# Every large matmul of an attention and FFN kernel split into two 64-row tiles that swap PSUM banks halfway

## The chip, the cores and the metric

The kernel runs on one core of a Trainium2 chip. The metric is the device time of one execution in microseconds, here the median of three runs. TensorE is called PE, VectorE DVE, ScalarE ACT, GpSimd POOL and SyncE SP, as in the profile.

## The reference

Block-sparse attention over 4 batches, 8 heads, 768 positions and a head dimension of 64, and after it a gated feed-forward layer over the 3072 tokens. Inputs and output are float32.

```python
scores = scale * np.matmul(q, k.transpose(0, 1, 3, 2))      # scale 1/8
# mask: neighbouring blocks of 32, first and last block, and 3 sampled blocks per block row
scores = np.where(mask, scores, -1e9)
scores = scores - np.max(scores, axis=-1, keepdims=True)
attn = np.exp(scores)
attn = attn / (np.sum(attn, axis=-1, keepdims=True) + 1e-09)
x = np.matmul(attn, v)                                        # heads joined: (3072, 512)
gate = 1.0 / (1.0 + np.exp(-(x @ w_gate)))                    # (512, 1536)
val = x @ w_val
out = (gate * val) @ w_out                                    # (1536, 512)
```

## The kernel before

The work is cut into 12 **units**: 4 batches times 3 groups of 256 query positions (`UQ`). All operands on PE are float16, all sums float32 in PSUM. PSUM has eight banks of 512 float32 columns.

**Attention of a unit.** Heads go in pairs, four pairs to a unit, and a pair has three steps (class `Step`). A step computes the scores of two heads for 256 keys and 256 queries, transposed, with keys on the partitions (`qk`, L460): four matmuls that contract over 64 rows, two for each head. The two heads lie on partitions 0 to 63 and 64 to 127, so each two matmuls use the two row halves of the PE array and write different PSUM banks. ACT takes the exponential of the two banks in one instruction (`exp`, L470), and DVE multiplies by the 0/1 mask (`mul`, L476). In the first unit the mask is added on PE as a bias instead (L452). `Pair.pv` (L498) multiplies the probabilities by the values, 24 matmuls of 65 columns for a pair, whose 65th column is the sum of the probabilities; DVE takes the reciprocal and scales (`norm`, L508 and L510). The result is transposed into `xT`, on PE in the first two units (L519), by a DMA transpose on SP's queue (L551) later.

**FFN of a unit** (class `Ffn`). `f` (L618) makes one of 12 chunks of 128 hidden features: four matmuls with the gate weights and four with the value weights, each contracting 128 rows, 256 columns, both in the two halves of one bank. ACT takes the tanh of the gate half (L629) and DVE forms (tanh + 1) times value (L634) into `ht`. `y` (L658) makes 128 tokens of the output in 12 matmuls of 512 columns; ACT (L695) copies them out with a factor 0.5 and SP's queue stores them. The very last tile goes out in two halves (`last`, L679 on ACT and L682 on DVE).

**The order.** The order of the instructions is made at build time by `Plan`: every piece of work is a task with the engines that may do it, a cost in microseconds written by hand, what it depends on, and the PSUM buffers that it takes and frees. `Plan.run` goes through time; whenever an engine is free it gives it the first ready task whose buffers are free, and so fixes the buffer too. The instructions are then issued in that order, and each engine runs its own list in order. A task that stands in the list waits for its semaphores, and all behind it on the same engine wait with it.

**PSUM.** There are two kinds of buffers, and the planner hands them out separately:

```python
plan = Plan({'m': 4, 's': 2})
spare = [ps.tile([128, 512], f32, name=f"m{i}") for i in range(4)]
score = [ps.tile([128, 2, 2, UQ], f32, name=f"s{i}") for i in range(2)]
```

The scores of a step take one of two `s` buffers of two banks; `pv`, `f`, `y`, the transposes and the mask tiles take one of four `m` buffers of one bank. The scores of two steps are issued together, except in the first two units (`scores`).

The FFN of a unit runs while the attention of the next unit is computed; their tasks are listed alternately in six slots (`parts`). At the start the queries, keys and values of batch 0 and then the FFN weights are loaded on POOL's queue, and the block mask is built: DVE and ACT copy mask tiles from PSUM (`mask_tile`, L348 and L235).

Of the kernel before, what the change touches and what calls it, by code (L numbers as in the profile page):

```python
# [25 lines left out]
DM = H * D  # L26
# [11 lines left out]
VW = 96  # L38

# [12 lines left out]
class Bank:  # L52
    def __init__(self, kind):
        self.kind, self.slot = kind, None


class Plan:
# [6 lines left out]
    def __init__(self, banks):  # L64
        self.tasks = []
        self.room = {kind: [(0.0, i) for i in range(n)] for kind, n in banks.items()}
# [5 lines left out]
    def run(self):  # L72
# [11 lines left out]
        while events:  # L84
            now, i = heapq.heappop(events)
            if i >= 0:
                for bank in self.tasks[i][5]:
                    self.room[bank.kind].append((now, bank.slot))
                for j in after[i]:
                    left[j] -= 1  # L90
                    if not left[j]:
                        bisect.insort(ready, j)
            if events and events[0][0] <= now:
                continue
            for eng in busy:
                if busy[eng] > now:
                    continue
                for j in ready:
# [4 lines left out]
                    kinds = [bank.kind for bank in take]  # L103
                    if any(len(self.room[x]) < kinds.count(x) for x in kinds):
                        continue
                    for bank in take:
                        oldest = min(self.room[bank.kind])
                        self.room[bank.kind].remove(oldest)
                        bank.slot = oldest[1]
# [5 lines left out]
                    order.append((eng, fn))  # L115
# [3 lines left out]
        for eng, fn in order:  # L119
            fn(eng)  # L120
        return end
# [3 lines left out]
def kernel(  # L125
# [132 lines left out]
    plan = Plan({'m': 4, 's': 2})  # L258
    spare = [ps.tile([128, 512], f32, name=f"m{i}") for i in range(4)]
    score = [ps.tile([128, 2, 2, UQ], f32, name=f"s{i}") for i in range(2)]  # L260
# [29 lines left out]
    def warm(n):  # L290
        for _ in range(n):
            nc.tensor.matmul(spare[3], junk[:, 0:128], junk, start=True, stop=True)
# [5 lines left out]
    bank = Bank("m")  # L298
# [24 lines left out]
    def more_rows():  # L323
        bank = Bank("m")
# [16 lines left out]
    def mask_tile(c0, c1, t):  # L341
        n = c1 - c0
        w = 512 // n
        bank = Bank("m")
# [21 lines left out]
    def prep(src, dst, b, p, t0, t1, deps, at):  # L366

        bank = Bank("m")
# [69 lines left out]
    class Step:  # L438
# [6 lines left out]
        def qk(self):  # L445
            b, u, p = self.b, self.u, self.p
            masked = (b, u) != (0, 0)
            for i in range(2):
                t = 2 * self.j + i
                if not masked:  # L450
                    for o in (0, D):
                        nc.tensor.matmul(  # L452
                            score[self.bank.slot][:, o // D, i, :],
                            e64[o : o + D, t * 128 : (t + 1) * 128],
                            bias[o : o + D, :],
                            start=True,
                            stop=False,
                        )
                for o in (0, D):
                    nc.tensor.matmul(  # L460
                        score[self.bank.slot][:, o // D, i, :],
                        kT[b % 2][o : o + D, p, t * 128 : (t + 1) * 128],
                        qT[b % 2][o : o + D, p, u * UQ : (u + 1) * UQ],
                        start=masked,
                        stop=True,
                    )

        def exp(self, eng):
            self.pt = work.tile([128, 2, 2, UQ], f16, tag="P", bufs=3 * VB, name="pt")
            nc.scalar.activation(  # L470
                self.pt, score[self.bank.slot], AF.Exp, bias=0.0, scale=SCALE
# [11 lines left out]
    class Pair:  # L483


        def __init__(self, n, p):
# [4 lines left out]
            self.bank, self.bank2 = Bank("m"), Bank("m")  # L491

        def pv(self, s):
            acc = spare[self.bank.slot][:, 0 : 4 * (D + 1)]
            self.acc = acc.rearrange("a (s h d) -> a s h d", s=2, h=2)
            for a in range(2):
                for t in range(NT):
                    nc.tensor.matmul(  # L498
                        self.acc[:, s, a, :],
                        self.steps[t // 2].pt[:, a, t % 2, s * 128 : (s + 1) * 128],  # L500
                        vex[self.b % 2][:, 2 * self.p + a, t, 0 : D + 1],
                        start=(t == 0),
                        stop=(t == NT - 1),
                    )

        def norm(self, eng):
# [4 lines left out]
                self.x16,  # L511
# [20 lines left out]
        def value(self):  # L532
            a = plan.add(
                [(PE, 0.41)],
                lambda eng: self.pv(0),
                self.products + [vdone[self.b, self.p]],
                take=[self.bank],
                lag=0.0,
            )
            a = plan.add([(PE, 0.41)], lambda eng: self.pv(1), [a])  # L540
# [30 lines left out]
    def scores(run):  # L571
# [10 lines left out]
        if first:  # L582
            deps.append(t_bias)
        a = plan.add(
            [(PE, 0.1 + (0.44 if first else 0.22) * len(run))],
# [14 lines left out]
    class Ffn:  # L600
# [7 lines left out]
        def f(self, f):  # L608
# [3 lines left out]
            def mm(eng):  # L612
                if f == 0:
                    self.ht = work.tile([128, NF, UQ], f16, tag="ht", bufs=2, name="ht")
                pg = spare[bank.slot].rearrange("a (i n) -> a i n", i=2)
                for i, w in enumerate((wg, wv)):
                    for c in range(4):
                        nc.tensor.matmul(  # L618
                            pg[:, i, :],
                            w[:, c, f * 128 : (f + 1) * 128],  # L620
                            xTs[self.n][0][:, c, :],
                            start=(c == 0),
                            stop=(c == 3),
                        )

            def tanh(eng):
                th = work.tile([128, UQ], f32, tag="th", bufs=4, name="th")
                box.append(th)
                nc.scalar.activation(  # L629
                    th, spare[bank.slot][:, 0:UQ], AF.Tanh, bias=0.0, scale=0.5  # L630
                )

            def gate(eng):
                nc.vector.scalar_tensor_tensor(  # L634
                    self.ht[:, f, :],
                    in0=box[0],
                    scalar=1.0,
                    in1=spare[bank.slot][:, UQ : 2 * UQ],
# [4 lines left out]
            deps = xdone[self.n] + (ring("ht", 2) if f == 0 else [])  # L643
            a = plan.add([(PE, 0.88)], mm, deps, at=land["w", f // 3], take=[bank])
            if f == NF - 1:
                used["xT"].append(a)
            c = plan.add([(ACT, 0.36)], tanh, [a] + ring("th", 4))
# [255 lines left out]
```

## Time and profile before

| | |
|---|---|
| runs | 297.08, 297.65, 297.1 us; median 297.1 us |
| span of the profiled execution | 294.5 us; 2.6 us less than the median, and no total of its own is recorded |
| granted TensorE clock | 0.999 |
| PE | 287.0 us busy, 3302 matmuls |
| ACT | 205.2 us busy, of it 139.8 us in 144 exponentials (L470) |
| DVE | 191.2 us busy, of it 91.0 us in 132 mask products (L476) |
| DMA | 28.55 MB read, 6.29 MB written |

The span runs from the first to the last instruction of the trace; the timed runs also hold what lies around it. Busy PE time is counted from modelled ends of pipelined matmuls that overlap, so the rows of the chain (start, length, engine, line, number of instructions) are the better guide: they follow PE from one start to the next.

### The profile page before, as it was taken

The page shows a single profiled execution, that of the slowest core. Times are in us where ns is not written, and L with a number is a line of the kernel's source. Part 1 is how long each engine was busy: PE and PEld are TensorE (multiplying, and loading weights), DVE is VectorE, ACT ScalarE, POOL GpSimd, SP SyncE. Part 2 cuts the span into 40 slices and gives each one's busy share as a digit, 9 for nine tenths or more (in the row PEclk, how much of TensorE's full clock was granted, in tenths as well). Part 3 has the DMA queues.
Part 4 walks back from the last instruction along what each step waited for, and adds up shares of the span by engine and source line. Part 5 has one row for each costly group of instructions (what it writes and reads, how often), then busy time and mean ns, then how long its engine had stood idle before and what let it go on. Part 6 is the DMA issues. An engine that isn't in the chain of part 4 may idle for free.

```text
span 294.5 us, 7862 instructions
## 1 busy us (share of the span) xinstructions
PE 287.0 (97%) x3302; PEld 203.8 (69%) x3302; DVE 191.2 (65%) x439; ACT 205.2 (70%) x323; POOL 48.3 (16%) x65
## 2 busy tenths in 40 slices
PE   7998999999999999999999999999999999999994
PEld 2656785785785786786776786786686687687771
DVE  3688878775675677675676577577477477475240
ACT  2789977677677677677677677777777777672431
POOL 8944100197000000197000000000000000000000
PEclk9999999999999999999999999999999999999999
DMA  7999999999910200999910203910200200201102
GB/s 115 190 201 204 205 206 203 215 150 146 222 16 23 79 11 10 191 171 143 220 24 12 81 11 70 214 43 20 80 11 20 80 11 20 80 13 20 71 2 71
DMA packets 74540, 28.55 MB, mean 97 GB/s; under 512 B 57352, under 2 KB 71560, under 8 KB 74504
## 3 DMA queue, kind: packets, MB, share of 16 engines
q0 software_dynamic: 40400, 14.16, 43.4%
q1 hardware_dynamic: 33924, 13.75, 20.8%
q8 instruction: 26, 0.43, 0.6%
q10 hardware_dynamic: 180, 0.13, 0.1%
q14 instruction: 10, 0.08, 0.1%
HBM read 28.55 MB, written 6.29 MB: 118 GB/s over the span
## 4 chain that ended last, share of the span: by engine, by line
PE 93%; ACT 3%; DVE 1%; DMA 1%; issue 0%; ACTq 0%; POOLq 0%
PE m L618 44%; PE m L658 22%; PE s L460 13%; PE m L498 11%; ACT pt L470 2%; DMA k<-in_k_dram 1%; PE m L383 1%; PE s L452 1%; ACT kT L233 1%; PE m L348 1%; ACT qT L233 0%; PE m L519 0%; DVE pr L374 0%; DVE pt L476 0%; DVE kT L235 0%
## 5 line engine op out<-in xcount | busy, mean ns | idle before, releaser
L470 ACT ACTIVATE pt<-s 128x1024 f16<-128x1024 f32 x144 | 139.8, 1023 | 7.8 <-PE s L460 7.7
L476 DVE TENSOR_TENSOR pt<-pt,mask 128x1024 f16<-128x1024 f16 x132 | 91.0, 690 | 51.7 <-ACT pt L470 51.7
L618 PE MATMUL m<-xT,wg 128*128 128x256 f16 x576 | 86.9, 273 | 0.3 <-DVE x L510 0.3
L629 ACT ACTIVATE th<-m 128x256 f32<-128x256 f32 x144 | 54.3, 388 | 46.6 <-PE m L618 46.0
L618 PE MATMUL m<-xT,wv 128*128 128x256 f16 x576 | 86.4, 273 | 0.0
L634 DVE SCALAR_TENSOR_TENSOR ht<-th,m 128x256 f16<-128x256 f32 x144 | 56.6, 416 | 20.7 <-ACT th L629 20.4
L658 PE MATMUL m<-wo,ht 128*128 128x512 f16 x288 | 66.1, 380 | 0.0
L618 PEld LDWEIGHTS <-wv 128*128 128x128 f16 x576 | 56.4, 98 | 6.5
L618 PEld LDWEIGHTS <-wg 128*128 128x128 f16 x576 | 50.6, 98 | 14.7 <-issue 9.7
L658 PEld LDWEIGHTS <-ht 128*128 128x128 f16 x288 | 26.5, 98 | 32.8 <-issue 4.2
L460 PE MATMUL s<-qT,kT 64*128 64x256 f16 x576 | 47.3, 273 | 1.1 <-ACT pt L470 0.8
L498 PEld LDWEIGHTS <-pt 128*128 128x128 f16 x1152 | 41.3, 97 | 3.8 <-issue 0.6
L498 PE MATMUL m<-vex,pt 128*128 128x65 f16 x1152 | 43.0, 193 | 0.0
L460 PEld LDWEIGHTS <-kT 64*128 64x128 f16 x576 | 23.0, 95 | 17.3 <-issue 13.6
L695 ACT ACTIVATE ysb<-m 128x512 f32<-128x512 f32 x23 | 13.7, 597 | 23.7 <-PE m L658 23.7
L741 POOL DMA_DIRECT2D kp<-in_k_dram x16 | 13.0, 820 | 78.2 <-DMA kT<-kp 51.1
L510 DVE TENSOR_TENSOR x<-m,rz 128x256 f16<-128x256 f32 x48 | 20.4, 424 | 1.7
L508 DVE RECIPROCAL rz<-m 128x4 f32<-128x4 f32 x48 | 8.7, 181 | 13.4 <-PE m L498 13.4
L741 POOL DMA_DIRECT2D qp<-in_q_dram x16 | 13.0, 819 | 2.9 <-DMA kp<-in_k_dram 1.3
L452 PE MATMUL s<-bias,e 64*128 64x256 f16 x48 | 6.7, 299 | 0.1
L235 DVE CAST mask<-m 128x512 f16<-128x512 f32 x9 | 5.7, 683 | 0.3 <-PE m L348 0.2
L383 PE MATMUL m<-ident,pr 128*128 128x128 f16 x48 | 4.9, 250 | 0.9 <-DVE pr L374 0.6
(45 smaller groups left out, 67.5 us busy)
## 6 DMA issues: line engine op xcount, KB each, us to landing
out_dram<-ysb SPq DMA_DIRECT2D x23, 256.0 KB, 2.0
v<-in_v_dram POOLq DMA_DIRECT2D x3, 768.0 KB, 10.4
wg<-in_moe_w_gate_dram POOLq DMA_DIRECT2D x4, 384.0 KB, 12.7
wv<-in_moe_w_val_dram POOLq DMA_DIRECT2D x4, 384.0 KB, 13.8
wo<-in_moe_w_out_dram POOLq DMA_DIRECT2D x3, 512.0 KB, 17.2
kp<-in_k_dram POOLq DMA_DIRECT2D x16, 96.0 KB, 6.7
qp<-in_q_dram POOLq DMA_DIRECT2D x16, 96.0 KB, 5.5
k<-in_k_dram POOLq DMA_DIRECT2D x4, 192.0 KB, 5.2
```

Of the source, the lines that this page charges most:

```text
L452: nc.tensor.matmul(score[self.bank.slot][:, o // D, i, :], e64[o : o + D, t * 128 : (t + 1) * 128], bias[o : o + D, :], start=True, stop=F ...
L460: nc.tensor.matmul(score[self.bank.slot][:, o // D, i, :], kT[b % 2][o : o + D, p, t * 128 : (t + 1) * 128], qT[b % 2][o : o + D, p, u * U ...
L470: nc.scalar.activation(self.pt, score[self.bank.slot], AF.Exp, bias=0.0, scale=SCALE)
L476: nc.vector.tensor_tensor(self.pt, self.pt, m.unsqueeze(1).broadcast_to([128, 2, 2, UQ]), op=ALU.mult,)
L498: nc.tensor.matmul(self.acc[:, s, a, :], self.steps[t // 2].pt[:, a, t % 2, s * 128 : (s + 1) * 128], vex[self.b % 2][:, 2 * self.p + a, t ...
L510: nc.vector.tensor_tensor(self.x16, self.acc[:, :, :, 0:D], rz.broadcast_to([128, 2, 2, D]), op=ALU.mult,)
L618: nc.tensor.matmul(pg[:, i, :], w[:, c, f * 128 : (f + 1) * 128], xTs[self.n][0][:, c, :], start=(c == 0), stop=(c == 3),)
L629: nc.scalar.activation(th, spare[bank.slot][:, 0:UQ], AF.Tanh, bias=0.0, scale=0.5)
L634: nc.vector.scalar_tensor_tensor(self.ht[:, f, :], in0=box[0], scalar=1.0, in1=spare[bank.slot][:, UQ : 2 * UQ], op0=ALU.add, op1=ALU.mult,)
L658: nc.tensor.matmul(spare[bank.slot], self.ht[:, f, s * 128 : (s + 1) * 128], wo[:, f, :], start=(f == 0), stop=(f == NF - 1),)
L695: nc.scalar.activation(ysb, spare[bank.slot], AF.Copy, bias=0.0, scale=0.5)
L741: nc.gpsimd.dma_start(dst[:, p, :, a, :], src[b, 2 * p + a].rearrange("(n t) d -> n t d", t=NT),)
```

## The change

Every matmul that contracted 128 rows of the attention's values, of the FFN's first layer and of its second layer becomes two matmuls of 64 rows, on the two row halves of the array. [...] So work is taken in two outputs that lie in two banks: in the first half of the work, row half 0 adds to the first bank and row half 1 to the second; in the second half they change places. Before the change of places PE waits for its own last matmul of the first half (`turns`); the planner is told a lag `GAP` for it and may put other work between.

PSUM becomes four shared units of two banks. A step's scores, `pv`, `f` and `y` each take a whole unit; transposes and mask tiles take a single bank, by preference one whose neighbour is taken. At most two units (`SCORES`) hold scores. `pv` has its two heads in the two banks. `f` makes two chunks of 128 features at a time, gate in one bank and value in the other, so tanh and product have 512 columns instead of 256 and are half as many. `y` makes both 128-token tiles of a unit at a time; both are copied out after its last matmul, the tail included (`last` is gone). Every step's scores are a task of their own. The order in which the parts of the FFN are listed is kept, with pairs of chunks in place of chunks.

```diff
+SCORES = 2
+GAP, PV_HALF, F_HALF, Y_ONE = 0.3, 0.36, 0.875, 0.216
...
+class Room:
...
+    def find(self, kind, free):
+        if kind == "1":
+            found = [(i ^ 1 in free, free[i], i) for i in free]
+        else:
+            found = [(max(free[i], free[i + 1]), i) for i in range(0, 8, 2) if i in free and i + 1 in free]
+        return min(found)[-1] if found else None
...
-    plan = Plan({'m': 4, 's': 2})
-    spare = [ps.tile([128, 512], f32, name=f"m{i}") for i in range(4)]
-    score = [ps.tile([128, 2, 2, UQ], f32, name=f"s{i}") for i in range(2)]
+    plan = Plan(SCORES)
+    units_ps = [ps.tile([128, 2, 512], f32, name=f"m{i}") for i in range(4)]
+    spare = [units_ps[i // 2][:, i % 2, :] for i in range(8)]
...
+    def turns(mms, bank, first, begins=True, ends=True):
+        if not first and begins:
+            tc.add_manual_dep(
+                nc.tensor.nop().ins,
+                bank.last.name,
...
+        for n, job in enumerate(mms):
+            for row in range(2):
+                out, lhsT, rhs = job(row if first else 1 - row, slice(row * D, (row + 1) * D))
+                bank.last = tiled(
+                    out, lhsT, rhs,
+                    first and begins and n == 0,
+                    not first and ends and n == len(mms) - 1,
+                ).ins
...
-            self.bank, self.bank2 = Bank("m"), Bank("m")
+            self.bank, self.bank2 = Bank("m"), Bank("1")
...
             a = plan.add(
-                [(PE, 0.41)],
-                lambda eng: self.pv(0),
+                [(PE, PV_HALF)],
+                lambda eng: self.pv(True),
                 self.products + [vdone[self.b, self.p]],
                 take=[self.bank],
-                lag=0.0,
+                lag=GAP,
             )
-            a = plan.add([(PE, 0.41)], lambda eng: self.pv(1), [a])
+            a = plan.add([(PE, PV_HALF)], lambda eng: self.pv(False), [a])
...
-            deps = xdone[self.n] + (ring("ht", 2) if f == 0 else [])
-            a = plan.add([(PE, 0.88)], mm, deps, at=land["w", f // 3], take=[bank])
...
-            c = plan.add([(ACT, 0.36)], tanh, [a] + ring("th", 4))
-            g = plan.add([(DVE, 0.41)], gate, [c], free=[bank])
+            a = plan.add(
+                [(PE, F_HALF)], half(True), deps, at=land["w", 2 * j // 3], take=[bank], lag=GAP
+            )
+            a = plan.add([(PE, F_HALF)], half(False), [a], at=land["w", (2 * j + 1) // 3])
...
+            c = plan.add([(ACT, 0.57)], tanh, [a] + ring("th", 3), free=[(bank, 0)])
+            g = plan.add([(DVE, 0.68)], gate, [c], free=[(bank, 1)])
...
+            for f0 in range(0, NF, 4):
+                a = part(False, f0, a)
+            used["ht"].append(a)
+            for s in range(2):
+                plan.add([(ACT, 0.6), (DVE, 0.69)], evac(s, 0, DM, nc.sync), [a], free=[(bank, s)])
...
-        for i in range(4):
-            parts.append([lambda F=F, f=f: F.f(f) for f in range(3 * i, 3 * i + 3)])
-        parts.extend([[lambda F=F, s=s: F.y(s)] for s in range(2)])
+        for js in ((0, 1), (2,), (3, 4), (5,)):
+            parts.append([lambda F=F, j=j: F.f(j) for j in js])
+        y = F.y()
+        parts.extend([[lambda y=y: next(y)] for _ in range(2)])
...
-            if n == 1:
-                for x in run:
-                    scores([x])
-            else:
-                scores(run)
+            for x in run:
+                scores([x])
```

## The prediction

> **What bounds the kernel now.** I read the page first, then the chain of waits, then single windows. The busy times and the chain's shares by engine:
>
> ```profile
> PE 287.0 (97%) x3302; PEld 203.8 (69%) x3302; DVE 191.2 (65%) x439; ACT 205.2 (70%) x323; POOL 48.3 (16%) x65
> ...
> PE 93%; ACT 3%; DVE 1%; DMA 1%; issue 0%; ACTq 0%; POOLq 0%
> ```
>
> PE sets the end, and after the first 27 us it never waits for data, so only its own stream counts: what a start costs, and what lies between two starts. The chain in order of time gives both (start, length, line, number of instructions):
>
> ```profile
> 53.53 0.98 PE m L618 x8
> 54.51 0.73 PE m L498 x24
> 55.24 1.75 PE m L618 x16
> 56.99 0.54 PE s L460 x8
> 57.53 2.73 PE m L618 x24
> ...
> 267.24 2.62 PE m L618 x24
> 269.86 5.18 PE m L658 x24
> 275.04 10.48 PE m L618 x96
> ```
>
> 96 matmuls of 256 columns take 10.48, so 0.109 each; 24 of 512 columns 5.18, 0.216 each; 24 of `pv` 0.73, 0.030 each. The 24 matmuls after scores take 2.73 instead of 2.62, the 8 after scores 0.98 instead of 0.87. And the eight score matmuls take 0.54: two at a time, four steps of 0.109 are 0.44, and 0.10 are left. So every change between 64-row and 128-row work costs about 0.105 us, going in and coming back. That is what the chain hides inside PE's 93%.
>
> Two more views are needed below, ACT in the startup and the end of the chain:
>
> ```profile
> 13.63 1.02 ACT L470 ACTIVATE pt<-s 128x1024 f16<-128x1024 f32 x1 [0.36 <-PE s L460]
> 14.82 0.80 ACT L233 COPY kT<-m 128x768 f16<-128x768 f16 x1 [0.17 <-PE m L383]
> 15.52 2.86 ACT L470 ACTIVATE pt<-s 128x1024 f16<-128x1024 f32 x3
> 18.63 1.94 ACT L470 ACTIVATE pt<-s 128x1024 f16<-128x1024 f32 x2 [0.25 <-PE s L460]
> 20.89 1.02 ACT L470 ACTIVATE pt<-s 128x1024 f16<-128x1024 f32 x1 [0.32 <-PE s L460]
> ```
>
> ```profile
> 285.52 5.19 PE m L658 x24
> 290.71 0.02 issue
> 290.74 0.39 ACT ysb L679
> 291.13 0.02 issue
> 291.15 0.42 DVE ysb L682
> ```
>
> Two exponentials in a row start 0.92 apart (1.94 for two, 1.02 for one), which needs two score buffers; and the last copies run one after the other, DVE behind ACT.
>
> **What goes: the changes of tiling.** In the PE order of the two programs I counted the places where 64-row and other work meet: 160 before, 36 after (those around the transposes, the bias and the mask tiles of the first 55 us). 124 x 0.105 = 13.0 us saved.
>
> **What stays: the streams.** 1152 matmuls of 256 columns become 1152 pairs, 288 of 512 columns become 288 pairs, 1152 of 65 columns become 1152 pairs. The score matmuls show a pair of 256 columns at 0.109, the price of one 128-row matmul, so I cost the FFN at nothing. Pairs of 65 columns are in no row. If they overlap as the score pairs do, 0.030 each and nothing changes (it could be 0.001 less, so -1 us); if the two ran one after the other, 1152 x 0.030 = 35 us more. The row nearest in kind, the score pairs, overlaps in full, and the weight loads of `pv`, 97 ns long, already run 0.030 apart; I take nothing and keep both ends.
>
> [...] No row here shows narrow pairs.
>
> **What is added: the change of places.** There are 132 (72 in `f`, 12 in `y`, 48 in `pv`). Uncovered, the second half starts when the last matmul's row has ended (0.273) and a semaphore has passed (about 0.06: in the window at 102 us the exponential starts that much after the fourth score matmul's row ends), instead of 0.109 after its start: 0.22. In the changed order 128 have other PE work of 0.22 us or more between the halves (a `pv` half 0.37, one or two steps of scores 0.22 or 0.44, a half of `f` 0.87). Four have none, two in the startup and two at the end: 0.9 us. Without that cover 132 x 0.22 = 29 us.
>
> **What is added: four units instead of four banks and two score buffers.** This is where I expect the gain to go. I laid the changed order out for one round of the middle (the attention of one unit, the FFN of the one before) with the durations of these rows; for 512 columns I take DVE's mask cast, 0.68, and ACT's copy in L695, 0.60. PE stands in three places:
>
> - *The start of `y`* takes the unit that `pv` has just left. From the last `pv` matmul: its row 0.19, passing 0.02, the reciprocal until the product may start 0.22, the product 0.42, passing 0.05, so 0.90; on PE the two steps of scores between cover 0.45. Wait 0.45. Queued behind: the whole of `y`.
> - *The first `f` after `y`* takes the unit of `y`. Both copies come after `y`'s last matmul, and in the program DVE's waits for ACT's: row 0.38, ACT 0.60, DVE 0.68, passings 0.10, so 1.76; between lie the matmul itself, two `pv` halves and two steps, 0.22 + 0.73 + 0.44 = 1.39. Wait 0.37.
> - *The third `f`* takes the unit of the first. Its tanh stands on ACT behind the exponentials of two steps (2 x 0.92), then 0.60, a mask product on DVE and the gate 0.68: 3.75 after the first of these steps began, when PE is ready at 3.54. Wait 0.22.
>
> That is 1.04 a round, nearly what the round's twelve changes of tiling cost (1.26). Ten rounds: 10.4 us. Fewer and wider tanh and gate instructions take 54.3 to 43 us off ACT's and 56.6 to 49 off DVE's list (72 x 0.60, 72 x 0.68); neither engine sets the end, so that earns nothing.
>
> **The startup.** Mask tiles and transposes take single banks, and `pv` a whole unit, so for some microseconds one unit is left for scores. Behind the eighth exponential PE's list now holds mask tiles, one of which waits for DVE's second mask cast, and behind it the second half of `pv` and only then the ninth step. From DVE's copy of the mask rows: 0.70 to the first cast, 0.60 to the second, 0.68 until it ends, 0.05, a mask matmul with its change 0.32, the `pv` half 0.37, scores and passing 0.64: 3.4, where the exponentials before ran 0.9 to 1.3 apart. The eighth and ninth come 1.7 further apart than before. The next step has one unit: scores 0.44, passing 0.20, exponential 1.02, 0.05, so 1.71 instead of 0.92, 0.8 more. By the thirteenth exponential I get 3.0 us, and a similar, smaller wait in the second unit, for which I take 1.0 (between 0 and 2): 4.0 us. Weights land no later than before, so nothing absorbs this.
>
> **The tail.** The last copies grow from 0.39 and 0.42 to 0.60 and 0.68, still one behind the other: 0.47. Two stores of 256 KB on SP's queue, 2.0 us to land, replace one of 128 KB there, 1.7: 0.3. Together 0.8.
>
> **Sum**, against the span of 294.5: -13.0 + 0.9 + 10.4 + 4.0 + 0.8 = +3.1; by rounding up the small passings that I left out in ten rounds (a step of scores that waits some 0.04 for its unit) +3.5. Span 298.0; with the 2.6 us between span and median, 300.6 us.
>
> **The rivals.**
>
> *Faster: the unit waits stay short.* The three waits are differences of long chains; if DVE and ACT come free 0.3 earlier than my layout has them, only the wait before `y` is left, with a rest of 0.45 a round. Then -13.0 + 0.9 + 4.5 + 4.0 + 0.8 = -2.8: 294.3 us. For it: ACT and DVE are idle for 30% and more. Against: each chain is serial, and the tanh is behind exponentials by PE's own order. It decides at 0.73 a round, where the sum is zero.
>
> *Slower: waits grow beyond the cover.* If a change of places takes 0.06 more on PE than counted (a weight load that cannot be drawn ahead past a wait), 132 x 0.06 = 8 us at most if nothing covers it, or half of it: 305 us. It decides where a cover is only just long enough, 0.22 and 0.36 under `f`.
>
> *Much slower: pairs of 65 columns do not overlap* or are bound by the doubled instructions (6604 weight loads and matmuls become 11788). At half of the bound 17 us, at the bound 35: 318 to 335 us. Against it: the score pairs.
>
> *The change does not do what it says:* if a 64-row pair of the FFN did not overlap, its 1152 would cost 125 us more. The score matmuls, same form and columns, exclude it.
>
> **How the numbers follow.** My sum, 297.8 to 303.5: 0.62. Faster rival, around 294: 0.16. Cover too short, around 305: 0.15. Narrow pairs: 0.07. The likeliest gives 300.6. The range leaves out the narrow pairs and the faster part of the first rival: 295.5 to 306.5. Within 0.2%, 0.6 us, is about what a measurement of this kernel can tell from no change. Faster by more: the faster rival less its edge, 0.14; the same, that edge and the lowest part of my sum: 0.06; slower, the rest: 0.80.
>
> **What would show it.** Right: the chain shows matmuls of the FFN after scores without the 0.1; PE waits for DVE (L510's and the gate's and the copy's lines) three times a round, 1 us together; the thirteenth exponential starts near 27.8 instead of 24.8 us; a round stays at about 22.4 us (now from 53.53 to 76.00 in the chain, 22.5). Wrong: a round under 22.0 (the waits are smaller), `pv`'s 24 pairs over 0.8 us (narrow pairs cost), or waits of PE for itself beyond 2 us in sum.

## The result, and the profile after

The changed kernel takes 306.07 us (median of 304.73 to 307.04) against 297.37 beside it: 1.0301 times as long, 95% interval 1.0265 to 1.0338. The forecast was 300.6 us. Executions more than 1.5% above the fastest of their kernel are left out of the ratios, which concerns two of experiment 6 alone. The profiled execution has a span of 305.1 us, 10.6 more than before. From its page:

```profile
PE 284.1 (93%) x5894; PEld 230.0 (75%) x5894; DVE 191.9 (63%) x377; ACT 190.6 (62%) x240; POOL 48.4 (16%) x65
...
PEclk9975999999999999999999999999999999999998
...
q8 instruction: 46, 0.75, 1.0%
...
PE 71%; DVE 12%; ACT 8%; issue 5%; DMA 2%; POOL 1%; ACTq 0%; POOLq 0%
```

PE still bounds the kernel, but its share of the chain fell from 93% to 71%. Two things were not looked for in the prediction: the clock row has a 7 and a 5 in the third and fourth slice (half clock from 19.1 to 29.4 us by the records; before, no drop after the first rise while PE works), and the instruction queue moves 46 packets where before it moved these:

```profile
q8 instruction: 26, 0.43, 0.6%
```

A round of the middle, from the chain in order of time (start, length, line, count):

```profile
84.25 3.76 PE m L315 x100
88.05 0.90 issue
88.95 1.03 ACT pt L547
90.00 0.69 DVE pt L553
90.69 0.61 DVE ht L717
91.34 7.33 PE m L315 x200
98.69 0.20 DVE rz L587
98.91 0.44 DVE x L589
99.39 5.81 PE m L315 x56
105.22 0.61 ACT ysb L767
105.85 0.70 DVE ysb L771
106.59 3.76 PE m L315 x100
```

From line to line this is what the prediction had drawn: the third `f` behind exponential, mask product and gate (L547, L553, L717), the start of `y` behind reciprocal and product (L587, L589), the first `f` after `y` behind both copies (L767, L771). From one `106.59` line back to `84.25` a round is 22.34, where before it was 22.47. By starts on PE, the three waits of such a round are 0.457, 0.407 and 0.218 us (forecast 0.45, 0.37, 0.22).

Where 10.6 us went, by the starts of PE's matmuls:

| part | before | after | difference |
|---|---|---|---|
| first `y` starts | 46.15 | 53.51 | +7.4 |
| nine rounds from there | 202.4 | 204.0 | +1.7: nine times -0.13, and two long rounds, 2.9 |
| the last two rounds | 36.84 | 37.25 | +0.4 |
| last `y` to the end | 9.2 | 10.3 | +1.1 |

In the startup the thirteenth exponential, the second of these three, starts at 31.47, and before at 24.80:

```profile
30.55 2.85 ACT L547 ACTIVATE pt<-m 128x1024 f16<-128x1024 f32 x3 [0.70 <-PE m L315]
```

Two rounds are too long, 23.53 and 24.07 us among 22.35. In the first, 0.32 belongs to transposes on PE that only this round has (experiments 3 and 9 have 22.67 and 22.68 there); the rest, 0.86 and 1.72, are stops. In the round above 200 matmuls run through in 7.33 us from 91.34; in the second long round the chain has the like piece broken:

```profile
136.04 3.76 PE m L315 x100
139.82 1.03 ACT pt L547
140.87 0.70 DVE pt L553
141.58 0.84 issue
142.42 2.67 PE m L315 x80
```

PE's last matmul before 142.42 had started at 140.60, in the middle of an `f` whose operands had all been there; the chain gives the time up to 141.58 to a mask product that ended meanwhile, and for the 0.84 left it finds nothing that PE waited for. An instruction packet, among the loads of q and k for the fourth batch, ran from 139.78 to 140.99, and PE went on 1.43 us after its end. Counted in PE's list of weight loads and matmuls, this stop and the one at 73.9 us (0.86) stand at the same place of every 256 instructions (number 193 and 195), and 0.75 MB in 46 packets are 16 KB each.

The traces of all runs agree. From 50 us on there are 20 stops of more than 0.3 us inside PE's stream that no wait for other work accounts for, in the changed kernel and eight of the kernels below. All of them stand at number 193 or 195 of 256, and in 19 of them PE goes on 1.3 to 1.6 us after the end of such a packet. In the middle rounds most packets start about when PE passes this place (in the changed kernel, 20 of the 30 from 100 to 285 us between number 178 and 216); the two before the stops here started 182 and 225 instructions after it.

The half clock, in windows of 3.4 us (columns: window; length; busy time and count of PE, PEld, DVE, ACT, POOL; clock; DMA share; GB/s):

```profile
15.71:19.12 3.41, 2.26 (x37) 0.99 (x33) 2.28 (x6) 2.49 (x4) 1.16 (x2) 1.00 1.35 201
19.12:29.36 10.24, 10.24 (x129) 5.94 (x129) 5.53 (x15) 4.57 (x6) 3.99 (x6) 0.50 1.34 202
```

In the first of them PE is "busy" for 2.26 us by its rows, but most of that is pipeline: matmuls times their spacing (0.109 for 256 columns and so on, a pair of 64-row matmuls counted once) make 0.50 of the window, and 0.26 if each counts by its rows of 128, since the mask matmuls have 24. The kernel before has at least 0.60 and 0.50 in every window after its clock has risen; this is its poorest by rows:

```profile
13.76:17.17 3.41, 3.29 (x38) 1.70 (x33) 3.17 (x10) 3.24 (x4) 2.62 (x5) 1.00 1.31 205
```

After that window the changed kernel's PE has a whole clock no more until 29.36.

### The profile page after: what moved, and what is told of

It is laid out like the page before. It is cut to its first block, busy times and chain, and to the rows that moved or that the text cites. A ratio compares the mean times of both kernels' runs of the same rounds, so it can differ in the third digit from the quotient of the medians.

```text
span 305.1 us, 12879 instructions
## 1 busy us (share of the span) xinstructions
PE 284.1 (93%) x5894; PEld 230.0 (75%) x5894; DVE 191.9 (63%) x377; ACT 190.6 (62%) x240; POOL 48.4 (16%) x65
## 4 chain that ended last, share of the span: by engine, by line
PE 71%; DVE 12%; ACT 8%; issue 5%; DMA 2%; POOL 1%; ACTq 0%; POOLq 0%
PE m L315 69%; ACT pt L547 5%; DVE pt L553 3%; DVE ysb L771 3%; DVE ht L717 2%; ACT ysb L767 2%; DMA k<-in_k_dram 2%; DVE x L589 2%; PE m L425 1%; PE m L460 1%; DVE rz L587 1%; DVE mask L284 1%; PE m L598 1%; POOL k L238 1%; POOL q L238 0%
## 5 line engine op out<-in xcount | busy, mean ns | idle before, releaser
L547 ACT ACTIVATE pt<-m 128x1024 f16<-128x1024 f32 x144 | 141.5, 1028 | 37.3 <-PE m L315 37.2
L315 PE MATMUL m<-xT,wg 64*128 64x256 f16 x1152 | 143.5, 269 | 5.1 <-DVE ysb L771 2.4
L315 PE MATMUL m<-xT,wv 64*128 64x256 f16 x1152 | 144.6, 269 | 0.0
L553 DVE TENSOR_TENSOR pt<-pt,mask 128x1024 f16<-128x1024 f16 x132 | 91.1, 691 | 49.4 <-ACT pt L547 46.2
L315 PEld LDWEIGHTS <-wv 64*128 64x128 f16 x1152 | 102.4, 94 | 10.8 <-issue 8.6
L315 PEld LDWEIGHTS <-wg 64*128 64x128 f16 x1152 | 104.1, 94 | 1.2 <-issue 0.2
L315 PE MATMUL m<-wo,ht 64*128 64x512 f16 x576 | 66.8, 376 | 3.6 <-DVE x L589 2.7
L315 PEld LDWEIGHTS <-ht 64*128 64x128 f16 x576 | 31.3, 94 | 31.9 <-issue 5.2
L315 PEld LDWEIGHTS <-pt 64*128 64x128 f16 x2304 | 50.8, 95 | 5.7 <-issue 1.8
L315 PE MATMUL m<-vex,pt 64*128 64x65 f16 x2304 | 53.4, 191 | 1.0 <-issue 0.7
L717 DVE SCALAR_TENSOR_TENSOR ht<-th,m 128x512 f16<-128x512 f32 x72 | 48.9, 680 | 8.4 <-ACT th L714 8.3
L315 PE MATMUL m<-qT,kT 64*128 64x256 f16 x576 | 49.4, 273 | 0.9 <-ACT kT L282 0.6
L587 DVE RECIPROCAL rz<-m 128x4 f32<-128x4 f32 x48 | 8.6, 180 | 21.4 <-PE m L315 21.3
L589 DVE TENSOR_TENSOR x<-m,rz 128x256 f16<-128x256 f32 x48 | 20.4, 425 | 1.7
L771 DVE TENSOR_SCALAR ysb<-m 128x512 f32<-128x512 f32 x12 | 8.3, 692 | 16.6 <-ACT ysb L767 16.6
L767 ACT ACTIVATE ysb<-m 128x512 f32<-128x512 f32 x12 | 7.2, 597 | 17.8 <-PE m L315 17.8
```

Of the source, the lines that this page charges most:

```text
L315: return nc.tensor.matmul(out, lhsT, rhs, start=start, stop=stop, skip_group_check=True)
L547: nc.scalar.activation(self.pt.rearrange("a h i n -> a (h i n)"), both(self.bank).rearrange("a h n -> a (h n)"), AF.Exp, bias=0.0, scale=SCALE
L553: nc.vector.tensor_tensor(self.pt, self.pt, m.unsqueeze(1).broadcast_to([128, 2, 2, UQ]), op=ALU.mult,)
L587: nc.vector.reciprocal(rz, self.acc[:, :, :, D : D + 1])
L589: nc.vector.tensor_tensor(self.x16.rearrange("a s h d -> a h s d"), self.acc[:, :, :, 0:D], rz.broadcast_to([128, 2, 2, D]), op=ALU.mult,)
L717: nc.vector.scalar_tensor_tensor(self.ht[:, 2 * j : 2 * j + 2, :].rearrange("a f n -> a (f n)"), in0=box[0], scalar=1.0, in1=both(bank)[:, ...
```

## The experiments

The medians of the kernel before lay between 296.8 and 297.4 us in the four series; each ratio is to the one beside it.

**1. Units of their own for the scores.**

```
+        if self.given < START:                    # START = 12 score buffers given back
+            free = {i: t for i, t in free.items() if (i < 4) == (kind == "s")}
```

> The changed kernel, but until twelve step's score buffers have been given back, the scores of the startup keep two of the four PSUM units for themselves and everything else (the masks, PV, the FFN's pairs) has the other two. Nothing of the work is left out. Theory (half clock): the 7.4 us that the changed kernel is late at its first y are two things, about 3.3 us in which PE waits for units while scores and masks share them, and about 4.1 us because PE, fed so thinly before 19 us, was granted half its clock from 19.1 to 29.4 us. With units of their own the scores do not wait behind masks; PE is fed again, the clock stays near 1.0 throughout, the 13th exponential starts at 26.5 to 27.5 us rather than 31.5, the first y at about 47 us rather than 53.5, and the time falls by about 6 us, to 300 us (299 to 302). Rival (the four shared units as such, no matter who takes them first): the clock drop is a consequence and costs nothing by itself, the waits for units only move; the first y stays within 1.5 us of 53.5 and the time at 305 to 306.5 us. Second rival (the whole loss is in the rounds): first y early, but the time above 304 all the same.

Measured: 305.33 us, 1.0287 (1.0245 to 1.0329): a miss. The clock still dropped, only earlier (half from 11.1 to 18.0 us); first `y` at 50.4, not 47. Two stops came to four, rounds of 23.75, 23.89, 23.10 and 23.41. Neither theory holds as it was put.

**2. Filling PE's idle time.**

```
+            for _ in range(JUNK.get((self.n, self.p), 0) if first else 0):   # {(0, 1): 6}
+                for row in range(2):
+                    r = slice(row * D, (row + 1) * D)
+                    tiled(both(self.bank)[:, row, :], junk[r, 0:128], junk[r, :], True, True)
```

> The changed kernel with its order and its units unchanged; only, six pairs of additional 64-row matmuls on spare data are put on PE at the head of the first PV half of the first heads, into a bank just taken and overwritten by the matmuls behind them, where PE would idle anyway. About 0.8 us of work is added and nothing is taken away. Theory (half clock): the clock is taken back because PE is too idle between 15.7 and 19.1 us; with that stretch filled, the granted clock is 1.0 from 20 to 30 us, the first y starts 3 to 4 us earlier (49.5 to 50.5 us, from 53.5), and the time falls to 302.8 us (302 to 304) although PE has more to do. Rival (the units alone make the startup late): the added work comes on top, the clock row may or may not change, the first y is at 53.5 or up to 0.8 us later and the time is 306 to 307 us.

Measured: 305.0 us, 1.0271 (1.0240 to 1.0301), again a miss: the clock had dropped before the filling, from 7.7 to 14.5 us, 6.8 us of half clock in place of 10.2; first `y` at 52.4, 1.1 us earlier in spite of 0.8 us more work. Where the clock drops differs from execution to execution; to fill one gap is not enough. In the three other executions the mean clock is 0.996 to 1.0, too high for a drop of 6.83 us, and their times, 303.4 to 305.23, are hardly better than the 305.25 of this one. Either a drop as early as this costs little, or the clock first rose later there, which the mean does not show.

**3. No late loads.**

```
-                pair_load(kp, k, b)
-                pair_load(qp, q, b)
-                load_heads(v16, v, b, 0, H)
```

> The changed kernel without the loads of q, k and v of the third and fourth batch: those batches compute on the data of the first two. Every instruction of PE, VectorE and ScalarE but the loads' own stays. In the changed kernel PE stops twice inside a stream without a wait for data, 0.86 us at 74 us and 1.81 us at 141 us, each beside a transfer of the instruction queue while q and k loads of 128-byte pieces run. Theory (PE runs out of instructions, because their transfer stands behind the loads): both stops vanish or shrink below 0.3 us each, and the time falls by 2 to 3 us, to 303 to 304 us; the startup and its half clock stay as they are (first y at 53 to 54 us). Rival (the stops come from the changed order itself, a bank or a weight load not seen): they stay where they are in the stream, and the time stays within 0.6 us of 306.

Measured: 304.78 us, 1.0265 (1.0228 to 1.0302); the profiled span 302.8, 2.3 less, with the same 10.2 us of half clock and the first `y` at the same 53.5. The rounds are 22.67, then 22.34 to 22.35 up to the seventh with 22.65: both stops are gone. The seventh round has a stop of its own, 0.54 us at 199.7, at number 193 of 256 like the others; its packet started late beside transposes and stores on SP's queue. The instruction queue moved the same 46 packets. So the two stops need the loads, and the changed order alone does not make them; but other transfers can make a short one.

**4. Both halves back to back.**

```
-                [(PE, PV_HALF)],
-                lambda eng: self.pv(True),
+                [(PE, 2 * PV_HALF + GAP)],
+                lambda eng: (self.pv(True), self.pv(False)),
```

(and in the same way the halves of `f`).

> The changed kernel, but the two halves of each PV pair and of each of the FFN's first-layer pairs stand directly behind one another on PE, so that the swap of the two banks in the middle of each has no other matmuls to cover it: 120 swaps, 72 of the FFN and 48 of PV (12 others, those of y, were uncovered before). Nothing of the work is left out. By the prediction's price of 0.22 us for a change of place without cover: 120 x 0.22 = 26 us at most, a time of 325 to 332 us; a part of it lies in waits that PE has anyway, so a forecast of 324 us. Rival (a swap costs PE nothing, since the second half's rows and columns are free by then): 305 to 308 us. Between them: each uncovered swap costs the difference divided by 120.

Measured: 322.63 us, 1.0876 (1.0853 to 1.0900). In a round of 24.02 us ten uncovered swaps, six of `f` and four of `pv`, each leave 0.224 us between starts: the forecast's price. They add 2.24 a round but the round grew by 1.67, because the 1.08 us of unit waits shrank to 0.41: the slower PE finds its units free. In its profile the clock rose at 13.8 us and did not drop, although the mask matmuls have 24 rows here; its poorest window by rows has 0.46. Its thirteenth exponential starts near the 27.8 of the prediction:

```profile
27.83 1.03 ACT L547 ACTIVATE pt<-m 128x1024 f16<-128x1024 f32 x1
```

**5. Masks on all rows.**

```
-    mb24 = sing.tile([NB, S], f16)
+    mb24 = sing.tile([128, S], f16)               # and a memset to 0
-                    e24[:, (t + i) * 128 : (t + i + 1) * 128],
+                    e64[:, (t + i) * 128 : (t + i + 1) * 128],
```

> The changed kernel, but the 24-row matmuls that spread the masks (12 of them between about 15 and 30 us) read 128 rows, the other 104 being zeros; one memset of VectorE is added at the start, and the count, order and length of everything else is the same. The first four runs left the clock as the suspect: every kernel of this family drops to half clock once in the startup, at different times (19 to 29 us, 11 to 18, 8 to 15), after a stretch of about 3.4 us in which PE streamed little and on few rows. Theory (the clock is granted by rows in use, and the half clock costs the time that PE runs in it): with the masks on all rows no stretch is below the mark, the clock stays at 1.0 from its first rise on, the first y starts 3 to 4 us before the 53.5 of the changed kernel, at 49.5 to 50.5, and the time is 302 to 303 us. Rival (rows don't count, or the clock's drop falls into waits for data and costs nothing): the time stays at 305 to 306.5 and the first y at 53 to 54.

Measured: 303.58 us, 1.0217 (1.0193 to 1.0241). The windows of this kernel over the stretch in question:

```profile
15.50:18.90 3.40, 2.29 (x38) 1.12 (x37) 2.27 (x6) 2.49 (x4) 1.66 (x3) 1.00 1.34 202
18.90:29.20 10.30, 8.85 (x200) 6.25 (x201) 7.73 (x20) 6.99 (x9) 3.87 (x5) 1.00 1.34 202
```

The thirteenth exponential, the second of two, starts at 28.04:

```profile
27.12 1.94 ACT L549 ACTIVATE pt<-m 128x1024 f16<-128x1024 f32 x2 [0.70 <-PE m L317]
```

The first of the two windows is nearly the same as in the changed kernel, 2.29 us for 38 matmuls against 2.26 for 37; but the clock stays, PE gets 200 matmuls done in the next 10.3 us instead of 129, and the first `y` starts at 49.9, not 53.5. So the half clock cost 3.6 us between these two executions. Other executions agree: the changed kernel and experiment 3, with masks of 24 rows, have mean clocks of 0.979 to 0.989 in all eight executions, this one 0.993 to 1.0 in all five; experiments 1, 2 and 6, with 24 rows in other orders, have some of each kind. The text above says that every kernel of the family drops once; experiment 4 did not. The time fell by less than 3.6, as the stops were longer in this profile (rounds of 23.58, 24.73 and 22.83: 4.1 us together, of it 0.32 the transposes of the first).

**6. One copy for y.**

```
-            for s in range(2):
-                plan.add([(ACT, 0.6), (DVE, 0.69)], evac(s, 0, DM, nc.sync), [a], free=[(bank, s)])
+            plan.add([(ACT, 0.93), (DVE, 1.15)], evac2, [a], free=[bank])    # 1024 columns
```

> The changed kernel, but both tiles of y leave PSUM by one copy of 1024 columns on whichever engine is free, where there were two of 512, the second of which waited for the first. By the prediction's step on unit waits, the first f after y waits 0.37 us because the unit of y comes free only when both copies are done; with one copy that wait falls to about 0.1, in 10 rounds, and so 2.5 to 3 us less than the changed kernel, 303 to 303.5 us, with rounds of 22.1 in place of 22.35. Rival (the unit that the first f takes is not the one that y holds, or the next wait is just as late): rounds stay at 22.35 and the time at 305 to 306.5.

Measured: rounds of 22.05, the wait of the first `f` after `y` down from 0.407 to 0.108, as expected. The times of the four executions are 300.18, 304.12, 304.84 and 307.93 us, and the ratio goes by the first two: 1.0168 (1.0111 to 1.0226). So the total says little of the forecast 303 to 303.5. Their mean clocks are 0.998, 0.985, 0.983 and 0.970 in the same order: one program, slower by 7.75 us where its clock stood half for longest. That one is the profiled execution, in which the clock dropped twice (11.4 to 18.3 and 21.7 to 31.9 us) and the first `y` came at 56.1.

**7. More changes of tiling in the kernel before.**

```
-            if n == 1:
-                for x in run:
-                    scores([x])
-            else:
-                scores(run)
+            scores(run[:1])
...
+                if i == 0:                         # behind the first FFN part
+                    scores(run[1:])
```

> The kernel before, but in each slice the second step's scores stand behind the first FFN part and not beside the first step's: 104 more changes between 64-row and 128-row tiling on PE, no other work more or less. By the prediction's price of 0.105 us a change: 104 x 0.105 = 10.9 us, a time of 307 to 308 us (from 296.8 to 297.4). Rival (a change of tiling costs PE nothing beyond the order of the work): 296 to 298 us. Rival (the first term of the sum was too large, for half of it lay in waits that PE has anyway): 302 to 303.

Measured: 307.28 us, 1.0349 (1.0323 to 1.0374), 10.06 more, or 0.097 for each of 104 changes. Its chain has one step of scores by itself wherever two stood together:

```profile
222.66 0.32 PE s L460 x4
222.99 0.98 PE m L618 x8
223.97 0.32 PE s L460 x4
224.29 1.85 PE m L618 x16
```

The four score matmuls take 0.32 where 0.22 is their stream, and the eight after them 0.98 where 0.87 is theirs. In this execution the clock rose at 4.8 us and did not drop: the order of before keeps it even where it rises early. It does so in nearly all executions, not all: of 46 of the kernel before that stand beside the experiments two have a mean clock of 0.985 and 0.986, too low for the last microseconds alone, with 297.87 and 297.80 us; the others have 0.993 or more.

**8. Everything at once, and a mistake.** Experiments 1, 5 and 6 together, extra warm-up matmuls, and the loads of the last two batches in 768-byte pieces:

```
-        if b == 1:
+        if True:                                   # every batch loaded as the second one is
```

> The changed kernel with everything that the runs so far blame taken away together: scores keep two units to themselves until twelve score buffers are back; masks on 128 rows, and three more warm-up matmuls at the start and three before the second head pair's transposes, against the half clock; y by one copy of 1024 columns; the loads of the third and fourth batch in 768-byte pieces with VectorE setting the head pairs side by side, as the second batch's are, against the stops for instructions; the second half of a pair planned 0.06 us later. Theory (the three causes are half clock, waits for units in the startup and behind y, and stops for instructions): first y at 46.5 to 47.5 us, rounds of 21.8 to 22.1, no stop above 0.3 us inside a stream, span 291 to 294, time 293 to 296 us: below the kernel before. Rival (something in the 64-row form itself costs time that none of these takes away): above 298 us, with rounds of 22.3 or more.

Measured: 331.04 us, 1.1131 (1.1090 to 1.1173). Rounds are 22.05 where nothing else happens, but two have 41.8 and 35.4. The chain from 60 us on:

```profile
59.10 24.85 DMA qT<-qp
```

q's transpose ran 24.85 us beside the 768-KB loads (the median of the changed kernel is 6.3), and PE stood 12.2 us for it. In the other long round PE stood 9.6 us for a transpose of x. There were still stops, up to 2.2 us: the larger pieces did not take them away here.

**9. Few loads at a time.** Experiment 5's kernel, and

```
+                    if len(issued) >= DEPTH:       # DEPTH = 3
+                        tc.add_manual_dep(nc.gpsimd.nop().ins, issued[-DEPTH].name, ...)
+                    issued.append(nc.gpsimd.dma_start(dst, src).ins)
```

> The kernel with the masks on 128 rows (the run before), so that the clock is whole, but the loads of q, k and v of the third and fourth batch are issued at most three at a time: a GpSimd instruction ahead of each waits until the load three before it has landed (v's load in four parts for that). In the kernel with the masks on 128 rows PE stops at 70.3 us (0.73), in the round of 142.9 us (2.22 at 137.1, and 0.5 later): rounds of 23.58, 24.73 and 22.83 us among others of 22.34, together 4.1 us too much. Theory (the transfer of PE's instructions stands behind loads already queued, and the 64-row form uses instructions up twice as fast): with three loads in flight in place of about nine the stops fall below 0.5 us each, all rounds lie within 22.3 to 22.8, and the time falls by 2.5 to 3.5 us from 303.6, to 300 to 301. Rival (it is not the loads' queue but the loads at all, or another thing): stops of the same sum, 303 to 304.5 us. Danger: landing later, the loads could make the transposes and so PE wait, above 304.

Measured: 302.07 us, 1.0170 (1.0150 to 1.0190). The rounds are 22.68 and then 22.35 eight times over: the same bytes and the same instructions, and no stop.

In its profile the clock was half from 9.5 to 12.9 us and the first `y` came at 50.9, so the gain on experiment 5 is 2.7 us in the span and 1.5 in the median.

**10 to 12. A version without the three causes.** Experiments 1, 5, 6 and 9 together, PV ahead of the FFN part and one pair moved to the fifth slice:

> The changed kernel with masks on 128 rows and six more warm-up matmuls (clock), loads of the third and fourth batch three at a time (instructions), y by one copy of 1024 columns, scores with two units to themselves until twelve score buffers are back, PV put ahead of the FFN part in its slice and one PV pair moved from the fourth slice to the fifth (waits for units). Theory (half clock, stops for instructions and waits for units are all that the changed kernel loses): no drop of the clock, first y at 47 to 49.5 us, rounds of 21.7 to 22.0 without the stops, so 49.5 + 10 x 21.85 + 17.1 + 10.3 = 295.4 at the most for the span's end and 293 to 297 us for the time, at or below the 297.2 of the kernel before. Rival (the 64-row form as such is slower): 299 us or more, with rounds above 22.2.

Measured: 299.53 us, 1.0076 (1.0043 to 1.0110): rounds of 21.84, but 3.5 us lost at 67 us, where PE waited for q's transpose of the second batch, which ran beside the next loads; after this wait the clock was half from 71.9 to 75.3 us. With three loads in flight there was still a stop of 0.56 us, at 92.2. With the head pairs prepared sooner and the loads behind that transpose:

> The kernel of the run before (all causes mended), with two waits taken out that its trace showed: 3.5 us at 67 us, where the first scores of the second batch waited for q's transpose, which had started 9 us after k's and ran beside the loads of the third batch. Here the head pairs are set side by side two at a time, and the loads of the third and fourth batch wait until that transpose has landed; and two warm-up matmuls fewer stand at the start. Theory (half clock, stops for instructions and late transposes were what was left): all rounds at 21.84 us, no stop over 0.5 us after 50 us, first y at 48 to 49.5, time 294 to 296 us, below the 296.9 to 297.2 of the kernel before. Rival (the wait moves to the next batch, or the clock drops elsewhere): 297 to 300.

Measured: 295.54 us, 0.9942 (0.9919 to 0.9965). All nine rounds are 21.84. And with the last `y` in its old form:

> The same kernel, but y of the last unit in the form of the kernel before: each tile's 12 matmuls on 128 rows in one bank after the other, the first tile's copy beside the second's matmuls, the last copy in two halves on ScalarE and VectorE. By the prediction's tail step (+0.8 us for two copies one after the other behind the last matmul, and an uncovered change of place of 0.22), last y to end falls from about 10.6 to 9.3 to 10 us, and the time by 0.4 to 1.2 us from the kernel beside it. Rival (the first tile's matmuls wait for the last gate, which the swap's first half hid no better): no difference within 0.3 us.

Measured: 294.66 us, 0.9913 (0.9888 to 0.9938): faster than the kernel before by 2.8 us. Last `y` to end went from 10.7 to 10.0 us. In the profiled executions the startup was shorter by 1.3 too, and a stop of 0.61 us at 90.9 came on top. These three kernels change the order of the work as well as the three causes, so they show that the 64-row form can reach the time of before, not what each cause is worth. Its page:

```profile
PE 278.5 (95%) x5874; PEld 220.8 (75%) x5874; DVE 185.6 (63%) x369; ACT 194.0 (66%) x239; POOL 52.5 (18%) x71
...
PEclk9999999999999999999999999999999999999999
...
PE 82%; ACT 8%; DVE 4%; issue 2%; DMA 2%; POOL 1%; ACTq 0%; POOLq 0%
```

## Why the prediction was right and wrong

The direction was right and most terms hold; the sum was 5.5 us short, because two costs were no term of it at all.

- *What goes, the changes of tiling.* Right in kind, a little too dear: 0.094 by starts on PE (0.097 in experiment 7) in place of 0.105, so 11.7 us and not 13.0.
- *What stays, the streams.* Right. 12 pairs of a `pv` half follow one another at 0.030; neighbouring starts are 9 to 21 ns apart for the most part, where the 65-column matmuls of the kernel before stood 29 to 35 ns apart. Of the score pairs of the kernel before most start 3 to 4 ns apart; most pairs of the changed kernel do not (16 to 21 ns). The rival on narrow pairs falls, and with it the guess that doubled instructions would be felt there.
- *The change of places.* Right: 0.22 forecast, 0.224 measured where uncovered, and covered in the changed order. The rival "cover too short" is out, though the time came out near its 305.
- *Four units.* Right to 0.04 us each: 0.457, 0.407 and 0.218 measured, 1.08 a round against 1.04. With the twelve changes of before at 0.094, 1.13 a round, the round stays about as good as it was: -0.13. About half of that is in the streams, as the pairs follow a little closer than the matmuls before (109.0 against 109.6 ns for 256 columns on average).
- *The startup.* This is the step that failed. It said 4.0 us by waits for units; measured 7.4. In the changed kernel the thirteenth exponential starts at 31.47, 6.7 after before (forecast 3.0). With no drop of the clock (experiment 5; it rises at 9.6 us there, at 10.3 in the kernel before) the first `y` is at 49.9, 3.8 after before, and the thirteenth exponential at 28.04, 3.2 after before; in experiment 4, whose clock did not drop either, it is at 27.83. So the waits came to what was laid out. What was missing is that PE, which waited so, with 24-row matmuls between the waits, was also granted half its clock from 19.1 to 29.4 us: 3.6 us by experiment 5. I had read the clock row of before as a constant.
- *The instructions.* The second missing term. The prediction counted 11788 weight loads and matmuls and asked only whether they slow down the narrow pairs. With them the instruction queue moved 46 packets, not 26, and where one came late, mostly beside loads, PE stopped until after its end: 0.86 and 1.72, together 2.6 us, in the profiled execution. Experiments 3 and 9, which take the loads or their number away, take these stops away, and PE's going on 1.3 to 1.6 us after a packet's end ties them to the packets. That PE had no instructions to run then is my reading of these times; no record says so.
- *The tail and the last rounds.* The tail was 1.1, forecast 0.8 and a swap of 0.22. The last two rounds cost 0.4 more than before: by starts PE stands 1.18 us in them, against 0.75 in the eight changes of tiling before. Two waits for units are 0.41 and 0.22, one swap without cover is 0.226 (the other such swap is that of the tail, both as forecast), and `y` waits 0.33 for the last gates, which was in no step.

Without half clock and stops the span would be 305.1 - 3.6 - 2.6 = 298.9, where the forecast had 298.0. Of the signs that the prediction named for "right" those of the rounds were there, a round of 22.35 among them; the one of the startup was not, as the thirteenth exponential started at 31.47 and not near 27.8. None of those for "wrong" was there: no sign had been named for what lies outside the sum.

Open are three things. What exactly the chip counts for the clock: over all kept profiles, in windows of 3.41 us that start where the records change, the share by rows is 0.39 or less in the eleven windows before a drop, and 0.37 or more in all that kept the clock. Without the weight by rows the two kinds do not part: three of the windows before a drop have 0.50 to 0.56, and windows of 0.37 to 0.46 kept the clock. That the rows count is thus well supported; the exact rule is not shown. Then, why only some packets start late. And why units of their own for the scores gain so little in the startup: 48.6 to 49.9 us in the last two kernels, with a whole clock, against 46.15 before.

## What to carry to other kernels

When a change makes PE wait in the startup, price the waits twice: once as time, and once as clock, for a PE that works thinly may pay half speed afterwards, as here, where 10.2 us at half clock came after 3.41 us that PE filled to 0.50; if the work in that stretch sits on few rows, try padding it with zeros to all rows, which added one memset here and, at a whole clock, no time on PE that shows (38 matmuls in 2.29 us of such a window, against 37 in 2.26). When a change multiplies PE's instructions, look at which loads run beside the densest streams, and try fewer of them in flight: with three, the rounds of experiment 9 were 22.68 and 22.35 throughout. Test a covered cost by taking the cover away, and read the single waits there: in experiment 4 the round grew by 1.67 where the swaps added 2.24, as other waits shrank from 1.08 to 0.41.

## What the runs showed of the hardware

The clock changed in steps of 3.41 us: 13.65 whole (four steps) and 10.24 half (three) in the changed kernel, 6.83 half (two) in experiments 1 and 2; at places that differ between executions of nearly the same program. The records of the changed kernel and of the one before hold two values, 1.0 and 0.5. In the seven windows before a drop in the startup PE's longest gap was 1.8 us.

The clock row counts the time before its first record as whole (1.00 up to 10.35 us in the kernel before). By the spacing of the matmuls it was not: in the timeline of the kernel before, pairs of bias and score matmuls (start, length, line) first stand 0.21 apart, and from 10.35 us on 0.11:

```profile
8.20 0.42 PE L452 MATMUL s<-bias,e 64*128 64x256 f16 x2
8.42 0.42 PE L460 MATMUL s<-qT,kT 64*128 64x256 f16 x2
...
10.46 0.27 PE L452 MATMUL s<-bias,e 64*128 64x256 f16 x2
10.57 0.27 PE L460 MATMUL s<-qT,kT 64*128 64x256 f16 x2
```

And PE stopped for up to 2.2 us (experiment 5, at 137.1 us), without a wait for other work, while loads of 96 KB in 128-byte pieces were under way (about nine in flight, as counted ahead of experiment 9). With at most three in flight there was no such stop in experiment 9, and one of 0.6 us in two of the last three kernels.

In all these kernels the matmuls of a 64-row pair write two different banks. A pair that writes one bank was not run; that the two halves need two is an assumption.
